# A new order of all steps in a gated FFT-convolution and MLP kernel, with the last output row in two pieces

## The chip, the cores and the metric

The kernel runs on one core of a Trainium2 chip. The metric is the device time of one execution in microseconds; several executions were timed, and their median counts. One further execution was recorded by the profiler, and all shares and durations below come from that one.

The engines are called as in the profile: PE is TensorE's matmul, PEld its weight load, DVE is VectorE, ACT is ScalarE, POOL is GpSimd and SP is SyncE, which in this kernel issues nearly all transfers (DMAs).

## The reference

The inputs have S = 2048 rows and D = 640 columns, and the MLP's inner width is F = 1536. All is bfloat16. `A_q` serves twice: as q of the first branch and as x of the second and of the gate.

```python
def _A_ref(q, k, v, shift_k, ssm_k, ssm_D):
    k_shift = sum(k_pad[:, t:t + S, :] * shift_k[:, ks - 1 - t] for t in range(4))   # four taps
    kv = k_shift * v
    kv_f, kf_f = rfft2(kv padded to 2S), rfft2(ssm_k padded to 2S)
    y = irfft2(kv_f * kf_f)[:S] + kv * ssm_D            # a convolution over all rows
    return q * y

def _B_ref(x, w1, w2, w3, w4):
    h = _gelu(_layernorm(x) @ w1)
    # four quarters of h's columns, shifted by +1, -1, +2, -2 rows
    x1 = x + concatenate([g0, g1, g2, g3]) @ w2
    return x1 + _gelu(_layernorm(x1) @ w3) @ w4

g = _sigmoid((x * gate_w).sum(-1))
out = g * _A_ref(...) + (1 - g) * _B_ref(...)
```

(The sum over taps and the padding are shortened here.)

## The kernel before

**Layout.** The 2048 rows stand as 128 partitions with 16 rows (`t1`) each; x, k, q and the output are worked on in four groups of four rows each (`c` = 0 to 3), 640 KB per group.

**Branch A.** `k_load` (L553) loads a group of k, and TensorE transposes it in three pieces (`transposed`, L618). `tap` (L574) makes the four-tap shift as products with diagonal matrices (`DG`) and multiplies by v. `v_load` loads v with indirect DMAs issued by POOL. The convolution is a Fourier transform in two stages, made of products with tables. `step1` (L409) is the first stage for kv (named `step1.KV.c`) and for the filter (`step1.HT0.c`, after `load_h` and `h_transpose`). Each step1 group makes two rows of 640 KB in SBUF, which are sent to DRAM (`S_x`, `S_h`; L434). `gather` (L437) reads them back in another arrangement. `step2` (L445) is the second stage, `product` (L479) multiplies the two spectra, `step3` (L494) goes back, again by way of DRAM (`S_g`), `gin` (L526) reads that, and `step4` (L861) makes the last stage and multiplies by q and by the gate.

**Branch B.** `x_stats` and `x_norm` make the layernorm: mean and variance on DVE or ACT, the power -1/2 on POOL, the scaling on DVE or ACT. `x_turn` (L635) transposes the result, groups 0 and 1 on TensorE and groups 3 and 2 by a transposing DMA. `mlp1` (L699) is W1 with its GELU on ACT, `w2` (L781) adds x, `x1_norm` (L793) is the second layernorm with a transposing DMA, `w3` (L828) has the second GELU and `w4` (L847) the last product. `w4` for one row makes 12 products of 512 columns and 12 of 128 columns into one PSUM tile, and DVE then works `ps * (1 - g) + x1` over all 640 columns (L854). The last operation of a row is DVE's addition of branch A (L889, the last part of `step4`). `store` (L844) writes two rows.

**What sets the order.** Nothing is scheduled by a tool. Every function above is cut into numbered parts, and one long string, `ORDER` (L893), lists all parts as `name.arguments:part`. The parts are issued in that order, each engine takes its own instructions from it, and every engine works its queue strictly in order. So the string sets the queue of PE, DVE, ACT, POOL and SP all at once. A letter in the arguments (`V` or `A`) says whether DVE or ACT does an evacuation or a norm; `D` means a DMA.

Buffers are set by hand as well. `SLOTS` (L66) gives the buffer of each allocation of a ring, in the order of the string: `c` four PSUM banks, `m` two wider PSUM tiles, `row` four SBUF buffers of 640 KB, which serve the loads of k, the normed rows, the step1 rows and q, and some smaller rings.

```python
def send(r):                                   # step1: one of the two rows of a group, L434
    SP.dma_start(out=scr[:, r, o:o + 4 * D], in_=stg[r][:])
...
for e in names:                                # emit: one entry of ORDER after the other
    n, k = e.split(":")
    ...
```

The opening of the string before the change is: a warm-up of TensorE with products of zeros (`warm`, L222, 11 matmuls and four times 3), the loads of x group 0, k 3, k 1 and k 2, then the next x and k 0, and only then W1; transposes of k and the first taps; the first `mlp1` after them.

Of the kernel before, what the change touches and what calls it, by code (L numbers as in the profile page):

```python
# [10 lines left out]
ALU = mybir.AluOpType  # L11
# [5 lines left out]
P = 128  # L17
# [12 lines left out]
def pieces(width):  # L30

    o = 0
    res = []
    while o < width:
        w = min(512, width - o)
        res.append((o, w))
        o += w
    return res
# [3 lines left out]
def kernel(  # L42
# [24 lines left out]
        "c": "012310320123102130120132013021320321010231302301203120321302103120302130213023012301203102310230"  # L67
             "123013201230312312010132013013012031023302131203012213020132030210312031023301230213102321003212"
             "130120310230132103210232031130220313120132002132013201323100231103232010123302130213021302130132"
             "0012301230123013213",  # L70
        "m": "01010101010101010101010101010101010101010101010101010101010101010101",
        "row": "01230132013120023102130213012030213030301",
        "gt": "012312002103120123012301201",
        "xt": "010101",
        "gq": "01210212012021012012101210110120120",
        "ax": "0123021302310312",
        "hp": "01231302",
# [98 lines left out]
    def flat(x):  # L176
        return x.rearrange("p t d -> p (t d)")
# [665 lines left out]

    def store(u):  # L844
        SP.dma_start(out=o_rows[:, 2 * u * D:2 * u * D + 2 * D], in_=flat(X1[:, 2 * u:2 * u + 2, :]))

    def w4(t1):  # L847
        c, i = t1 // 4, t1 % 4
        ps = slot(psm, [P, D], F32, "ps4", "m", 2)
        for (o, w) in pieces(D):  # L850
            for f in range(FC):
                PE.matmul(ps[:, o:o + w], lhsT=st["gt", c, f // 4][:, f % 4, i * P:(i + 1) * P], rhs=st["W4"][:, f, o:o + w], start=(f == 0), stop=(f == FC - 1))  # L852
            yield
        V.scalar_tensor_tensor(out=X1[:, t1, :], in0=ps[:], scalar=OMG[:, t1:t1 + 1], in1=X1[:, t1, :], op0=ALU.mult, op1=ALU.add)  # L854
# [6 lines left out]
    def step4(t1, ev):  # L861
# [240 lines left out]
```

## Time and profile before

| | us |
|---|---|
| median of 3 runs | 239.57 (239.03 to 241.48) |
| the profiled execution | 239.24 |
| its span | 237.5 |
| PE busy | 224.6 (95%) |
| DVE busy | 194.7 (82%) |
| ACT busy | 174.0 (73%) |
| POOL busy | 16.9 (7%) |
| mean granted clock of TensorE | 1.00 |
| bytes moved by DMA | 57.06 MB, mean 240 GB/s |

How to read it: the span runs from the first to the last instruction that the profiler recorded; the 1.74 us between it and the time of the profiled execution lie outside. Busy time counts an engine's instructions, not the issuing of DMAs. A share of busy time is an average over stages with different limits; which wait ends last in a stage is read from that stage.

### The profile page before, as it was taken

To read this page: it belongs to the slowest core of one execution; us is meant where nothing else is said; L and a number is where in the kernel's file an instruction comes from. 1 tells how busy PE (TensorE), PEld (TensorE's weight loads), DVE (VectorE), ACT (ScalarE), POOL (GpSimd) and SP (SyncE) were. 2 spreads that over 40 slices of the span, in tenths; PEclk is the share of its full clock that TensorE was granted. 3 is DMA by queue.
4 is the path that set the end of the run, shared out by engine and by line. 5 is a ranking of instruction groups with operands and counts; after the bars stand their busy time and mean duration, and the time that the engine had idled before them with its cause. 6 is when DMAs were issued, how large, how long until landed. Compare 5 with 4: busy or idle time off the path is not lost.

```text
span 237.5 us, 5627 instructions
## 1 busy us (share of the span) xinstructions
PE 224.6 (95%) x2241; PEld 115.8 (49%) x2260; DVE 194.7 (82%) x458; ACT 174.0 (73%) x311; POOL 16.9 (7%) x34
## 2 busy tenths in 40 slices
PE   8986999999999999999999999999999999999791
PEld 3764655533755555444544343444444445456551
DVE  7996999998998999875798897686895988129793
ACT  4796999878887989999697887673698533547560
POOL 4415022000000200021200000000000000000000
PEclk9999999999999999999999999999999999999999
DMA  6999919761999699996899902499950456399672
GB/s 248 375 391 353 359 60 197 182 246 56 382 354 294 212 361 208 353 385 261 286 278 190 354 1 89 130 272 317 360 163 5 139 196 198 138 272 369 190 276 110
DMA packets 42743, 57.06 MB, mean 240 GB/s; under 512 B 20313, under 2 KB 35418, under 8 KB 42462
## 3 DMA queue, kind: packets, MB, share of 16 engines
q1 hardware_dynamic: 42142, 54.10, 71.3%
q0 software_dynamic: 576, 2.62, 2.8%
q8 instruction: 17, 0.28, 0.5%
q14 instruction: 8, 0.07, 0.1%
HBM read 34.42 MB, written 18.36 MB: 222 GB/s over the span
## 4 chain that ended last, share of the span: by engine, by line
PE 87%; DMA 5%; DVE 3%; issue 2%; ACT 1%; SPq 0%; ACTq 0%
PE ps L834 22%; PE ps L852 20%; PE psm L709 10%; PE psw L786 9%; PE ps L462 5%; DMA WA<-in_B_w_dram 5%; PE ps L875 4%; PE ps L422 4%; PE psk L590 3%; PE ps L509 3%; PE psz L227 3%; PE ps L424 3%; PE pst L395 2%; PE pst L618 1%; DVE X L854 1%
## 5 line engine op out<-in xcount | busy, mean ns | idle before, releaser
L852 PE MATMUL ps<-W,gt 128*128 128x128 bf16 (+1 forms) x370 | 54.7, 296 | 1.2 <-issue 0.8
L834 PE MATMUL ps<-x1t,W 128*128 128x512 bf16 x240 | 55.6, 380 | 0.0
L852 PEld LDWEIGHTS <-gt 128*128 128x128 bf16 x384 | 29.0, 98 | 25.2 <-issue 4.9
L834 PEld LDWEIGHTS <-W 128*128 128x128 bf16 x240 | 21.9, 98 | 28.5 <-issue 4.7
L369 ACT CAST gs<-ps 128x320 bf16<-128x320 f32 x40 | 14.9, 433 | 20.4 <-PE ps L509 14.0
L369 ACT CAST stg<-ps 128x512 bf16<-128x512 f32 x46 | 24.8, 594 | 6.7 <-PE ps L424 3.7
L839 ACT ACTIVATE gt<-ps 128x1024 bf16<-128x1024 f32 x24 | 24.7, 1036 | 3.9 <-PE ps L834 3.8
L709 PE MATMUL psm<-xt,WA 128*128 128x512 bf16 x100 | 23.5, 380 | 1.8 <-DMA WA<-in_B_w_dram 1.8
L371 DVE CAST stg<-ps 128x512 bf16<-128x512 f32 x34 | 22.5, 684 | 2.1 <-PE ps L422 1.3
L786 PE MATMUL psw<-WA,HT 128*128 128x128 bf16 (+1 forms) x112 | 21.1, 296 | 0.4 <-issue 0.2
L879 ACT ACTIVATE y<-ps,GS 128x320 bf16<-128x320 f32 x23 | 11.5, 527 | 8.7 <-PE ps L875 6.4
L369 ACT CAST hs<-ps 128x512 bf16<-128x512 f32 x25 | 13.6, 598 | 3.4 <-PE ps L462 3.4
L371 DVE CAST XS<-ps 128x512 bf16<-128x512 f32 x17 | 11.3, 685 | 5.6 <-PE ps L462 5.6
L369 ACT CAST XS<-ps 128x512 bf16<-128x512 f32 x23 | 12.6, 595 | 4.2 <-PE ps L462 4.1
L709 PEld LDWEIGHTS <-WA 128*128 128x128 bf16 x100 | 9.0, 98 | 13.3 <-DMA WA<-in_B_w_dram 2.0
L371 DVE CAST hs<-ps 128x512 bf16<-128x512 f32 x15 | 10.1, 688 | 6.6 <-PE ps L462 6.5
L371 DVE CAST gs<-ps 128x320 bf16<-128x320 f32 x24 | 11.1, 486 | 5.2 <-PE ps L509 4.7
L786 PEld LDWEIGHTS <-HT 128*128 128x128 bf16 x116 | 10.0, 98 | 10.5 <-issue 0.8
L854 DVE SCALAR_TENSOR_TENSOR X<-ps,OMG,X 128x640 bf16<-128x640 f32 x16 | 14.0, 877 | 0.6 <-PE ps L852 0.6
L462 PE MATMUL ps<-ax,CMP 64*32 64x512 bf16 (+3 forms) x512 | 12.9, 300 | 0.1
L885 DVE SCALAR_TENSOR_TENSOR q<-ps,GS,q 128x320 bf16<-128x320 f32 x9 | 4.8, 546 | 10.0 <-PE ps L875 10.0
L788 DVE SCALAR_TENSOR_TENSOR X<-psw,X 128x640 bf16<-128x640 f32 x16 | 12.9, 818 | 0.2
(150 smaller groups left out, 362.6 us busy)
## 6 DMA issues: line engine op xcount, KB each, us to landing
S_x<-stg SPq DMA_DIRECT2D x8, 640.0 KB
S_h<-stg SPq DMA_DIRECT2D x8, 640.0 KB
ax<-S_x SPq DMA_DIRECT2D x8, 640.0 KB
ax<-S_h SPq DMA_DIRECT2D x8, 640.0 KB
S_g<-gs SPq DMA_DIRECT2D x8, 640.0 KB
W<-in_B_w_dram SPq DMA_DIRECT2D x2, 1920.0 KB
kn<-in_A_k_dram SPq DMA_DIRECT2D x4, 640.0 KB
q<-in_A_q_dram SPq DMA_DIRECT2D x4, 640.0 KB
```

Source lines behind the costliest of these rows:

```text
L369: A.copy(out=dst, in_=src)
L371: V.tensor_copy(out=dst, in_=src)
L422: PE.matmul(ps[r][:], lhsT=F1N[:, r].rearrange("p a b -> p (a b)"), rhs=src[:, o + 512 * u:o + 512 * u + 512], start=True, stop=True)
L462: PE.matmul(ps[j][q:q + 32, lo - 512 * u:hi - 512 * u], lhsT=CMP[HALF[j], 8 * b + 4 * h + i, c, :], rhs=st[name, 2 * b + h][HALF[j], i, lo ...
L709: PE.matmul(ps[:, v, :].rearrange("p (a b) -> p a b", a=4), lhsT=W1N[:, k, 160 * f:160 * f + P] if f < 4 else W1M[:, k, :], rhs=xt[:, :, k ...
L786: PE.matmul(ps[:, o:o + w], lhsT=h_tile(f, t1), rhs=W2P[:, f, o:o + w], start=(f == 0), stop=(f == 4))
L788: V.scalar_tensor_tensor(out=X1[:, t1, :], in0=ps[:], scalar=1.0, in1=X[:, t1, :], op0=ALU.mult, op1=ALU.add, accum_out=S12[:, 0, t1:t1 + 1])
L834: PE.matmul(ps[:, u, :].rearrange("p (a b) -> p a b", a=4), lhsT=st["W3"][:, k, f * P:(f + 1) * P], rhs=xt[:, :, k, :], start=(k == 0), st ...
L839: A.activation(out=gt[:, 2 * (fp % 2):2 * (fp % 2) + 2, :], in_=ps[:], func=ACT.Gelu_apprx_tanh)
L852: PE.matmul(ps[:, o:o + w], lhsT=st["gt", c, f // 4][:, f % 4, i * P:(i + 1) * P], rhs=st["W4"][:, f, o:o + w], start=(f == 0), stop=(f == ...
L854: V.scalar_tensor_tensor(out=X1[:, t1, :], in0=ps[:], scalar=OMG[:, t1:t1 + 1], in1=X1[:, t1, :], op0=ALU.mult, op1=ALU.add)
L879: A.activation(out=box["y"][:], in_=box["ps"][:], func=ACT.Copy, scale=GS[:, t1:t1 + 1])
```

## The change

Three things are changed.

1. The string `ORDER` is written anew from the first entry to the last. The parts are the same, apart from the last row of `w4` and one more store. The choice of engine (`V` or `A`) of many evacuations changes with it. In the opening, the loads are issued as x group 0, x group 1, k 3, W1, k 1, k 2, x 3, k 0; the layernorm, turning and W1 products of x group 0 stand ahead of most of k's transposes and of all taps; W2's load comes much later; `load_q.2` stands in the middle of the kernel, among the gathers. `gather.x.6` stands ahead of the first send of `step1.HT0.3`, and the transposing load of `x1_norm.0` ahead of the second.
2. `SLOTS` is written anew to go with it.
3. `w4` for row 14 (`LAST`) uses two single PSUM banks, one for 512 and one for 128 columns, and has an operation of its own for each on DVE; and `store` writes the last two rows one by one.

The opening of the string and the places that are spoken of, before and after:

```diff
-  "... load_x0.0:0 ... load_x0.1:0 ... k_load.3.AAA:0 ... k_load.1.VAA:0 ... k_load.2.VAV:0 ... load_cj:0 ... load_x.1:0 k_load.0.AVV:0
-   ... tap.7.AA:0 ... load_w1:0 ... tap.9.VA:0 load_x.3:0 ... mlp1.0.1:0 ... load_w2:0 ... tap.5.AV:0 ... mlp1.0.0:0 ..."
+  "... load_x0.0:0 consts0:0 consts0:1 warm:0 load_x0.1:0 load_x.1:0 ... x_norm.0.AVVA:0 f4_table:0 k_load.3.AAA:0 ...
+   load_w1:0 k_load.1.VVA:0 ... x_turn.0.AAA:0 ... k_load.3.AAA:1 k_load.2.AVA:0 ... mlp1.0.0:0 ... mlp1.0.1:0 ... tap.7.AA:0 ..."
...
-  "step1.HT0.2.AAVAVAVAVA:16 ... gather.x.1:0 ... step1.HT0.3.AVAVAAVAAA:16 ... :15 ... x1_norm.0.AVVA:6 ... gather.x.7:0 ... gather.x.0:0 gather.x.6:0"
+  "step1.HT0.2.AAAAAVAAAA:16 ... gather.x.1:0 ... gather.x.6:0 ... step1.HT0.3.AVAAAAAAAA:16 ... x1_norm.0.VVVV:6 ... step1.HT0.3.AVAAAAAAAA:15"
...
-  "... w4.14:0 ... store.3:0 store.5:0 ... w4.14:1 ... store.4:0 ... w4.14:2 step4.14.AA:6 store.6:0 store.7:0"
+  "... store.7:0 step4.13.AA:6 step4.12.AA:6 step4.14.AA:5 store.4:0 store.6:0 w4.14:0 w4.14:1 w4.14:2 w4.14:3 step4.14.AA:6 store.8:0"
```

and the code:

```diff
+    LAST = NT - 2
+
     def store(u):
-        SP.dma_start(out=o_rows[:, 2 * u * D:2 * u * D + 2 * D], in_=flat(X1[:, 2 * u:2 * u + 2, :]))
+        a, n = (2 * u, 2) if u < 7 else (22 - u, 1)
+        SP.dma_start(out=o_rows[:, a * D:(a + n) * D], in_=flat(X1[:, a:a + n, :]))

     def w4(t1):
         c, i = t1 // 4, t1 % 4
-        ps = slot(psm, [P, D], F32, "ps4", "m", 2)
+        ps = None if t1 == LAST else slot(psm, [P, D], F32, "ps4", "m", 2)
         for (o, w) in pieces(D):
+            to = slot(psc, [P, w], F32, "ps4", "c", 4) if ps is None else ps[:, o:o + w]
             for f in range(FC):
-                PE.matmul(ps[:, o:o + w], ...)
+                PE.matmul(to[:, 0:w], ...)
             yield
-        V.scalar_tensor_tensor(out=X1[:, t1, :], in0=ps[:], scalar=OMG[:, t1:t1 + 1], in1=X1[:, t1, :], op0=ALU.mult, op1=ALU.add)
+            if ps is None:
+                V.scalar_tensor_tensor(out=X1[:, t1, o:o + w], in0=to[:], scalar=OMG[:, t1:t1 + 1], in1=X1[:, t1, o:o + w], op0=ALU.mult, op1=ALU.add)
+                if o == 0:
+                    yield
+        if ps is not None:
+            V.scalar_tensor_tensor(out=X1[:, t1, :], in0=ps[:], scalar=OMG[:, t1:t1 + 1], in1=X1[:, t1, :], op0=ALU.mult, op1=ALU.add)
```

More of the change, by code (lines that the diff above doesn't have):

```diff
@@ L66 @@
     SLOTS = {
[L67 to L73, printed above, removed]
+        "c": "012301230213012310323103120132103123010320130213102321032103230120312013201320132031203102313201"
+             "203213021021323013203210312300123120231203123012130120313021323013223102103120310321032013212032"
+             "310230121303120301202130321231030122103032101231302031230123210123012031203103220133012301231023"
+             "103120312031201023102",
+        "m": "0100100101010101010101010101010101011010101010110101010101011010101",
+        "row": "01230121032130301230123102310320230202023",
+        "gt": "012301202120103102012301201",
         "xt": "010101",
-        "gq": "01210212012021012012101210110120120",
-        "ax": "0123021302310312",
-        "hp": "01231302",
+        "gq": "012201201102102101202102102101102101",
+        "ax": "0123023102130213",
+        "hp": "01231203",
     }
@@ L842, in scale_x1 @@
         scaled(ev, X1[:, t1, :], X1[:, t1, :], OMG[:, t1:t1 + 1])
+    LAST = NT - 2
     def store(u):
-        SP.dma_start(out=o_rows[:, 2 * u * D:2 * u * D + 2 * D], in_=flat(X1[:, 2 * u:2 * u + 2, :]))
+        a, n = (2 * u, 2) if u < 7 else (22 - u, 1)
+        SP.dma_start(out=o_rows[:, a * D:(a + n) * D], in_=flat(X1[:, a:a + n, :]))
     def w4(t1):
         c, i = t1 // 4, t1 % 4
-        ps = slot(psm, [P, D], F32, "ps4", "m", 2)
+        ps = None if t1 == LAST else slot(psm, [P, D], F32, "ps4", "m", 2)
         for (o, w) in pieces(D):
+            to = slot(psc, [P, w], F32, "ps4", "c", 4) if ps is None else ps[:, o:o + w]
             for f in range(FC):
-                PE.matmul(ps[:, o:o + w], lhsT=st["gt", c, f // 4][:, f % 4, i * P:(i + 1) * P], rhs=st["W4"][:, f, o:o + w], start=(f == 0), stop=(f == FC - 1))
+                PE.matmul(to[:, 0:w], lhsT=st["gt", c, f // 4][:, f % 4, i * P:(i + 1) * P], rhs=st["W4"][:, f, o:o + w], start=(f == 0), stop=(f == FC - 1))
             yield
-        V.scalar_tensor_tensor(out=X1[:, t1, :], in0=ps[:], scalar=OMG[:, t1:t1 + 1], in1=X1[:, t1, :], op0=ALU.mult, op1=ALU.add)
+            if ps is None:
[4 more added lines that the diff above has]
+            V.scalar_tensor_tensor(out=X1[:, t1, :], in0=ps[:], scalar=OMG[:, t1:t1 + 1], in1=X1[:, t1, :], op0=ALU.mult, op1=ALU.add)
     def load_q(c):
```

306 rows, old and new, of the table ORDER are left out of this document.

## The prediction

> **What bounds the kernel now.** I read the page's busy shares first, then the waits of TensorE, then windows of time, and then single instructions where the change moves something.
>
> ```profile
> PE 224.6 (95%) x2241; PEld 115.8 (49%) x2260; DVE 194.7 (82%) x458; ACT 174.0 (73%) x311; POOL 16.9 (7%) x34
> ...
> PE 87%; DMA 5%; DVE 3%; issue 2%; ACT 1%; SPq 0%; ACTq 0%
> ```
>
> TensorE (PE) is busy for 224.6 of 237.5 us and holds 87% of the chain that ended last. The change removes no product, so it can win only what PE now loses, and it can lose wherever a new wait stops PE. The waits of PE say where it stands still:
>
> ```profile
> PE psm L709 <- DMA WA<-in_B_w_dram: 1.8, 1, 1.8
> PE ps L875 <- DVE q L885: 1.2, 1, 1.2
> PE psz L227 <- DVE NPI L244: 1.0, 1, 1.0
> ...
> PE psk L590 <- ACT yk L598: 0.5, 1, 0.5
> ```
>
> There are two waits of size: 1.8 us for W1's load (WA) at 20.05, and 1.2 us in the last phase for DVE's gating of q. The rest of the loss is work without a product (warm-up matmuls, L227) and the tail after PE's last matmul. The windows (us; then busy PE, PEld, DVE, ACT, POOL, granted clock, share of DMA, GB/s):
>
> ```profile
> 10.00:20.00 10.00, 6.96 (x108) 5.61 (x105) 9.40 (x29) 9.84 (x16) 2.48 (x3) 1.00 1.03 392
> 20.00:30.00 10.00, 9.44 (x116) 6.36 (x117) 7.43 (x18) 7.51 (x14) 2.98 (x4) 1.00 1.04 344
> 30.00:60.00 30.00, 29.84 (x250) 13.50 (x250) 28.20 (x93) 26.77 (x49) 2.65 (x4) 1.00 0.57 152
> 60.00:76.00 16.00, 15.87 (x156) 10.52 (x156) 15.07 (x31) 12.88 (x22) 0.20 (x1) 1.00 1.02 364
> 76.00:95.00 19.00, 18.89 (x121) 9.95 (x121) 18.40 (x48) 17.79 (x37) 1.22 (x2) 1.00 0.86 246
> 95.00:120.00 25.00, 24.80 (x272) 11.15 (x273) 18.60 (x48) 22.45 (x40) 3.67 (x6) 1.00 0.91 323
> ```
>
> Three things stand here. PE loses 3 us of 10 in 10-20 and is full afterwards. DVE and ACT are also nearly full from 30 to 95, so a wait there is not made up by them. The DMA engines are saturated until 30 and again from 60 on, so the order of transfers decides when they land.
>
> **The opening (largest gain).** Before: by 26.29 us PE has done 100 transposes at 0.057 us (5.7), five taps of 22 matmuls at 0.92 (4.6) and ten W1 matmuls (2.3): 12.6 us of useful work, 13.7 us lost. From there to the q wait the loss grows no further. After: the loads are issued in the order x rows 0-3, next x, a k piece, then W1 (before: W1 was ninth, issued 9.27, landed 20.00). By the landing rate of before (640 KB in about 1.75 us) W1 lands near 11. The chain ahead of the first W1 product is then the layernorm: DVE's variance to 7.7, POOL's two rows (1.01 and 0.25 with gaps, to 9.3), four norms of 0.45 to 0.95 us on DVE and ACT (the first done at 10.3, the last near 11.5), 20 transposes, and the xt copies (1.02 and 0.60 us on ACT, 0.64 on DVE) to 13.3. Beside it PE does 40 transposes (2.3 us). So PE starts the W1 products at 13.35 with 2.3 us useful done: 11.05 lost against 13.7. In the next 13 us the taps' copies and the last x and k turns give waits like the rows of 0.3 to 0.5 us; I leave 0.4 for one. **-2.3** (-3.0 to -0.8). The four v loads go behind the third norm on POOL; the KV products that need them come after 30 us, which covers their 10 us. W2's load moves behind the transposing loads on SP; it is wanted some 5 us after its landing.
>
> **KV row 2 and the transposes of h.** The steps KV.2 with parts 9, 0 and 12 and the first transposes of h now stand back to back. The PSUM banks come round every 0.32 us (two 64-row matmuls), while a bank needs its evacuation (0.594 us on ACT, 0.684 on DVE) and two engines free a bank only every 0.32. The zero-row copies and four KV.1 copies stand ahead on ACT. Before, W2 products of 1.4 us lay between. Ends: 0, if the engines have caught up, and 1.0, two evacuations less the matmuls beside them; **+0.5**.
>
> **The row buffer at HT0.1.** Each 640-KB row of step1 (L409) is evacuated into one of four row buffers and sent from there. Before, this gave one wait, on ACT:
>
> ```profile
> L369 ACT CAST stg<-ps 128x512 bf16<-128x512 f32 x46 | 24.8, 594 | 6.7 <-PE ps L424 3.7 <-PE ps L422 1.7 <-DMA S_h<-stg 0.8
> ```
>
> It is the 0.82 us to 88.88, when the first send of HT0.3 had landed (88.80), and PE did not feel it. After, `gather.x.6` is issued ahead of that send: one more 640 KB, 1.75 us. And both engines now wait for the same buffer, DVE for part 11 and ACT for part 14. All sends are earlier by 2.3 - 0.5 = 1.8, so the buffer comes free near the old 88.8 (to 89.5), while PE is 1.8 ahead and wants it at about 87. PE has some 1.4 us of matmuls until it needs the bank; then the evacuation itself (0.69) is on the path: 88.8 - 87 - 1.4 + 0.69 = 1.1. Ends: 0 (as before) and 2.8 (one slower transfer more). The old row cost PE nothing, so I go below the middle: **+0.8**. What stands behind, the transposing load of `x1_norm.0` (landed 92.61, wanted 94.33) and gathers h.6 and h.7 (landed 116.53 and 118.34, wanted 117.69 and 118.86), has 0.5 to 1.7 us of slack that this stop gives back; 0 there.
>
> **The last phase.** `load_q.2` was issued at 212.53, behind the gin loads, and landed at 220.93; PE waited 1.23 at 220.4. Now it is issued near 125 and the wait goes. Against it, `load_q.0` and `gin.0.1` stand on SP between the last S_g send and `gin.0.2`, which the next step4 wants: 0 to 1.0 later, I take 0.3. The row `q.3` is wanted later than it lands by about 0.5. DVE's 8.23 of 10 us in 212-222 leaves a little for the moved gating; 0.2. -1.2 + 0.5 = **-0.7** (-1.2 to +0.5).
>
> **The tail.** Now the chain after PE's last matmul at 232.50 is:
>
> ```profile
> 232.53 0.88 DVE L854 SCALAR_TENSOR_TENSOR X<-ps,OMG,X 128x640 bf16<-128x640 f32 x1 [0.30 <-PE ps L852]
> 233.45 0.49 DVE L889 TENSOR_TENSOR X<-X,q 128x640 bf16<-128x640 bf16 x1
> ```
>
> then a store of 320 KB (issued 233.97, landed 236.13). Split, the 512-column operation lies beside the twelve 128-column matmuls (0.67 us), and only the 128-column one (estimate 0.3, from 0.877 for 640 and 0.546 for 320 columns) stays: -0.57. The last store holds one row, 160 KB: about -0.3 of its 2.16. **-0.9** (-0.5 to -1.1).
>
> **Evacuations** moved from DVE to ACT: about nine, 0.684 off DVE and 0.594 onto ACT each. PE has the same instructions. In the fullest stretch, 76-95, ACT has 1.2 us free and DVE 0.6, which covers the one or two that fall there; if it did not, each would cost what it takes on ACT. Priced at nothing beside the two terms above.
>
> Sum: 239.24 - 2.3 + 0.5 + 0.8 - 0.7 - 0.9 = 236.6. The profiled execution (span 237.5 and 1.74 outside it) is 0.33 below the median of 239.57; in its terms 237.0. A measurement of this kernel tells about 1% from no change, and 237.0 lies just below the 237.2 where that begins.
>
> **A rule on the clock.** All of this row's windows have a granted clock of 1.00, and the 1.81 us without a matmul at 18.2-20.05 were followed by ten W1 matmuls in 2.33 us, full pace. In the change the warm-up ends near 8.4, PE stands until 10.3 (1.9 us), and does only 2.3 us of small transposes in the next 3. If that cools the array, the first W1 products run at the pace of the first ten warm-up matmuls, which took 4.3 us (0.426 each; the next ten 0.215 each): ten or so of them, +2.1. The Trainium skill, "TensorE: Matmul & The Clock Gate", Part 1, says that the array falls back to half clock after an idle window of about 3.4 us, and rises after as long a busy one. By that rule 1.9 us alone keep it warm, as the trace of before agrees, but the sparse 5 us might not.
>
> **Rivals.**
> 1. The row buffer costs its whole price, 2.5 instead of 0.8: 238.7. For it: both evacuating engines stop at once and are over 93% busy there. Against: DMA has 14% free in 76-95. Chance 0.18.
> 2. The opening gains only 0.3: DVE and ACT are 94% and 98% busy in 10-20, and the W1 products add GELUs of 1.04 us to the same engines earlier. 239.0. Against: part of this work was there waiting, and PE's 13.35 is fixed by it already. Chance 0.10.
> 3. The clock falls in the opening: +2.1, 239.1. Chance 0.05.
> 4. Everything new hides (the +0.5 and +0.8 are 0): 235.7. Chance 0.06.
> 5. Slower: on SP the transposing load of `x1_norm.0` now stands ahead of HT0.3's second send. Before it held SP for 4.38 us (86.48 to 90.86), with that send ahead of it (issued 85.17, landed 90.34). If it holds SP as long, the send and all S_h sends behind it go 4 to 5 us later, into DMA queues that are full until 112; gathers h.6 and h.7 land near 121 to 123 instead of 116.5 and 118.3, and PE, with no slack there beyond 0.5 us, stands until then. The opening's gain is lost in it, and 4 us more: 239.24 + 4.2 - 0.7 - 0.9 = 241.8, 242.2 against the median. It decides from a landing of h.7 at 121 on; below it, the result is the forecast or rival 1. Against: the DMA queues are not empty during those 4.4 us, so what waits on SP loses less than that. Chance 0.16.
>
> **How the numbers follow.** The forecast has 0.45, of which 0.40 is below 237.2; with rival 4 that is 0.46 faster. Rivals 1 to 3 and the rest of the forecast make 0.38 within 1%. Rival 5 is 0.16 slower. Its own range: with the ends of the terms 234.9 to 239.0; the whole range reaches up to 241.2, leaving out most of rival 5, and down to 234.8.
>
> **What would show it.** Right: W1 landed near 11 and the first L709 at about 13.4; the wait on WA gone; no q wait above 0.5 us in step4; PE's last matmul within 0.5 us of the last 128-column STT. The row buffer would show as DVE and ACT idle on S_h near 88 and PE waiting on an evacuation there. Wrong: a first L709 after 15; PE idle over 2 us for a gather of S_h near 117; half-pace L709 at 13.

## The result, and the profile after

The changed kernel took 241.69 us (median of 14 runs, 241.15 to 242.78) against 239.59 us for the kernel before beside it: a ratio of 1.0091, 95% interval 1.0062 to 1.0119. In a later comparison (median of 4 runs) it was 242.98 us, ratio 1.0115 (1.0075 to 1.0155). The profiled execution took 241.72 us with a span of 239.9. The change made the kernel about 1% slower; 237.0 had been forecast, and the time lies above the range. The page of the changed kernel, busy time and the chain:

```profile
PE 227.0 (95%) x2260; PEld 115.2 (48%) x2260; DVE 191.6 (80%) x454; ACT 176.6 (74%) x318; POOL 17.6 (7%) x34
...
PE 71%; DMA 14%; ACT 8%; DVE 3%; issue 2%; POOL 1%; SPq 0%; ACTq 0%
```

PE held 87% of the chain before and holds 71% now; DMA and ACT have taken its place. The waits of PE (wait, sum, times, longest):

```profile
PE ps L422 <- ACT stg L369: 2.5, 3, 1.7
PE psz L227 <- DVE WZ L223: 1.9, 1, 1.9
PE pst L618 <- ACT xn L661: 1.6, 1, 1.6
PE ps L834 <- ACT gt L839: 1.0, 1, 1.0
...
PE ps L884 <- DMA gin<-S_g: 0.4, 1, 0.4
```

The two waits of before, for WA and for q, are gone. The new ones at the top and in the fourth line are in one place, as the windows show (same columns as before):

```profile
10.00:20.00 10.00, 9.90 (x107) 7.06 (x108) 9.64 (x31) 9.98 (x16) 4.32 (x6) 1.00 1.01 360
...
76.00:95.00 19.00, 16.54 (x105) 8.46 (x104) 14.11 (x38) 14.54 (x30) 1.78 (x2) 1.00 0.84 243
95.00:120.00 25.00, 23.78 (x231) 9.82 (x228) 18.31 (x42) 23.51 (x39) 2.43 (x4) 1.00 0.84 283
```

PE is busy for 9.90 of 10 us in 10-20, against 6.96 before. From 76 to 95 it has 16.54 of 19, against 18.89, and DVE and ACT too have fallen there, by 4.3 and 3.3 us. All three engines wait. The timeline of that place:

```profile
84.68 0.59 ACT L369 CAST stg<-ps 128x512 bf16<-128x512 f32 x1 [0.20 <-PE ps L422]
89.05 1.07 ACT L369 CAST stg<-ps 128x512 bf16<-128x512 f32 x2 [3.78 <-DMA S_h<-stg]
...
95.89 1.28 ACT L823 ACT_TABLE_LOAD   x1
...
100.20 1.28 ACT L839 ACT_TABLE_LOAD   x1
...
89.06 0.69 DVE L371 CAST stg<-ps 128x512 bf16<-128x512 f32 x1 [1.41 <-DMA S_h<-stg]
...
89.69 0.86 PE L422 MATMUL ps<-HT,F1N 128*128 128x512 bf16 x2 [1.68 <-ACT stg L369]
...
92.90 0.87 PE L422 MATMUL ps<-HT,F1N 128*128 128x512 bf16 x2 [0.56 <-ACT stg L369]
...
102.57 2.32 PE L834 MATMUL ps<-x1t,W 128*128 128x512 bf16 x10 [0.96 <-ACT gt L839]
```

ACT stands for 3.78 us until 89.05 and DVE for 1.41, both for the row buffer that the first send of HT0.3 still reads (issued 83.29, landed 88.97). PE stops 1.68 us later on. Then ACT is in arrears: PE waits for its copies at 92.90 and for its GELU at 102.57. And there is a line that the kernel before does not have: a table load for the Tanh of L823 at 95.89, with the GELU's own load after it at 100.20. In the kernel before the GELU's load came first, and the Tanh, behind it, had none:

```profile
96.39 1.28 ACT L839 ACT_TABLE_LOAD   x1
...
103.06 0.21 ACT L823 ACTIVATE GS<-ZG 128x16 f32<-128x16 f32 x1
```

To put numbers on places I use PE's lost time: the start of a step in the trace, less the durations of all PE work without the warm-up before it, each taken from the rows of before. It grows where PE stands or is slowed. Where the durations taken are a little too long it also falls slowly, in both kernels (from 13.19 to 11.44 between 122 and 200 in the kernel before), so only differences between kernels in the same row are read. (The stop in a pair of products is partly hidden in their longer modelled duration, 0.86 for 0.43, so lost time is more than the idle time in brackets.)

| after so much PE work (us) | before | after | after, second profile |
|---|---|---|---|
| 30 (opening) | 13.06 | 10.49 | 11.43 |
| 46, then 50 (KV.2) | 13.22, 12.90 | 10.56, 11.04 | 11.50, 11.99 |
| 76 | 13.23 | 11.37 | 12.29 |
| 78 (the stop) | 13.23 | 13.46 | 14.37 |
| 92 (its wake: what is lost behind it) | 13.60 | 16.52 | 17.43 |
| 122 | 13.19 | 16.82 | 17.63 |
| 200, then 216 (last phase) | 11.44, 12.34 | 15.13, 15.78 | 15.95, 17.05 |

(The second profile is that of the later comparison.) So 2.6 us are won in the opening (1.6 in the second profile), and 5.15 are lost between 76 and 92, where the kernel before lost 0.4.

### The profile page after: what moved, and what is told of

Its sections match the earlier page's. It is cut to its first block, busy times and chain, and to the rows that moved or that the text cites. A ratio compares the mean times of both kernels' runs of the same rounds, so it can differ in the third digit from the quotient of the medians.

```text
span 239.9 us, 5658 instructions
## 1 busy us (share of the span) xinstructions
PE 227.0 (95%) x2260; PEld 115.2 (48%) x2260; DVE 191.6 (80%) x454; ACT 176.6 (74%) x318; POOL 17.6 (7%) x34
## 4 chain that ended last, share of the span: by engine, by line
PE 71%; DMA 14%; ACT 8%; DVE 3%; issue 2%; POOL 1%; SPq 0%; ACTq 0%
PE ps L856 18%; PE ps L834 14%; PE psm L709 9%; DMA S_h<-stg 6%; PE psw L786 6%; PE psk L590 4%; PE ps L884 4%; PE ps L462 3%; PE pst L618 3%; PE ps L509 3%; ACT stg L369 3%; DMA ax<-S_h 3%; PE pst L395 2%; PE ps L422 2%; DMA gin<-S_g 2%
## 5 line engine op out<-in xcount | busy, mean ns | idle before, releaser
L856 PE MATMUL ps<-W,gt 128*128 128x512 bf16 (+1 forms) x384 | 56.8, 300 | 0.3 <-ACT gt L839 0.3
L369 ACT CAST stg<-ps 128x512 bf16<-128x512 f32 x56 | 29.8, 595 | 6.1 <-DMA S_h<-stg 3.8
L369 ACT CAST gs<-ps 128x320 bf16<-128x320 f32 x44 | 16.2, 440 | 18.8 <-PE ps L509 13.6
L371 DVE CAST stg<-ps 128x512 bf16<-128x512 f32 x24 | 15.9, 686 | 7.4 <-PE ps L422 3.6
L786 PE MATMUL psw<-WA,HT 128*128 128x512 bf16 (+1 forms) x116 | 21.7, 299 | 0.0
L369 ACT CAST hs<-ps 128x512 bf16<-128x512 f32 x25 | 13.5, 593 | 8.2 <-PE ps L462 8.2
L371 DVE CAST XS<-ps 128x512 bf16<-128x512 f32 x22 | 14.6, 685 | 4.4 <-PE ps L462 4.4
L786 PEld LDWEIGHTS <-HT 128*128 128x128 bf16 x116 | 10.0, 98 | 11.5 <-issue 2.5
L371 DVE CAST gs<-ps 128x320 bf16<-128x320 f32 x20 | 9.0, 485 | 7.8 <-PE ps L509 5.8
L422 PE MATMUL ps<-HT,F1N 128*128 128x512 bf16 x40 | 11.4, 379 | 2.7 <-ACT stg L369 2.5
L462 PE MATMUL ps<-ax,CMP 64*32 64x384 bf16 (+3 forms) x512 | 13.0, 300 | 0.2 <-DMA ax<-S_h 0.2
L712 ACT ACTIVATE HT<-psm 128x1024 bf16<-128x1024 f32 (+1 forms) x12 | 10.6, 895 | 2.4 <-PE psm L709 2.3
```

What stands on the lines that cost most here:

```text
L369: A.copy(out=dst, in_=src)
L371: V.tensor_copy(out=dst, in_=src)
L422: PE.matmul(ps[r][:], lhsT=F1N[:, r].rearrange("p a b -> p (a b)"), rhs=src[:, o + 512 * u:o + 512 * u + 512], start=True, stop=True)
L462: PE.matmul(ps[j][q:q + 32, lo - 512 * u:hi - 512 * u], lhsT=CMP[HALF[j], 8 * b + 4 * h + i, c, :], rhs=st[name, 2 * b + h][HALF[j], i, lo ...
L786: PE.matmul(ps[:, o:o + w], lhsT=h_tile(f, t1), rhs=W2P[:, f, o:o + w], start=(f == 0), stop=(f == 4))
L856: PE.matmul(to[:, 0:w], lhsT=st["gt", c, f // 4][:, f % 4, i * P:(i + 1) * P], rhs=st["W4"][:, f, o:o + w], start=(f == 0), stop=(f == FC ...
```

## The experiments

Ratios are to the kernel before, with the 95% interval; it took 240.07 to 240.34 us beside these runs. They were made in three sets, each with its own runs of the kernel before; times out of different sets are compared only roughly.

**One send behind one gather.**

```diff
-  ... gather.x.1:0 ... gather.x.6:0 ... step1.HT0.3.AVAAAAAAAA:16 ...
+  ... gather.x.1:0 ... step1.HT0.3.AVAAAAAAAA:16 gather.x.6:0 ...
```

> The changed kernel (241.69) with gather.x.6 issued behind the first send of step1.HT0.3 instead of ahead of it; nothing else. Theory W (the wait for the row buffer makes the loss): that send lands 1.75 us earlier, near 87.2; ACT's wait of 3.78 us shrinks to about 2, PE's first stop of 1.68 to near 0, and part of the wake behind it goes: 238.8 to 239.8. Rival A (ACT has too much work from 86 to 106 whatever the wait): 241.2. Rival D (the S_h gathers h.6 and h.7 set the pace near 117 to 122): PE gains and stands there instead, 241.0.

Measured: 241.05 us, ratio 1.0024 (0.9997 to 1.0051); the changed kernel's two medians lie 0.6 and 1.9 us above it. ACT's wait is cut to half, as expected, and the lost time between 76 and 92 falls from 5.15 to 3.20:

```profile
88.11 1.07 ACT L369 CAST stg<-ps 128x512 bf16<-128x512 f32 x2 [1.82 <-DMA S_h<-stg]
```

The wait is 1.96 us shorter, near the 1.75 of one 640-KB transfer. The time misses the 238.8 to 239.8 expected and is what the two rivals had given (241.2 and 241.0), so the time alone does not choose. In the trace PE waits only 0.2 us for h.6 and h.7, which speaks against rival D; rival A is left to the next experiment.

**A fifth row buffer.**

```diff
-  stg[r] = slot(ring, [P, 4 * D], BF16, "stg", "row", ROW)
+  if (name, c, r) == ("HT0", 1, 1):
+      stg[r] = pool("C").tile([P, 4 * D], BF16, name="stg5", tag="stg5", bufs=1)
+  else:
+      stg[r] = slot(ring, [P, 4 * D], BF16, "stg", "row", ROW)
```

> The changed kernel with a fifth row buffer: the second row of step1.HT0.1 goes to a buffer of its own, so no copy waits for the send of HT0.3; the order is untouched. Theory W: the waits of 3.78 us on ACT and 1.41 on DVE for S_h go, PE's 1.68 goes and most of the 3.1 us that PE loses behind it: 237.0 to 238.2, less if h.6 and h.7 then bind. Rival A: only the 1.7 goes, 240.0. Rival D: PE waits 3 us or more for h.6 and h.7, 240.5 or more.

Measured: 239.19 us, ratio 0.9948 (0.9919 to 0.9977). Nothing but the buffer is changed (and its entry in `SLOTS` taken out), and the time is 2.5 us under the first median of the changed kernel and 3.8 under the second. The window:

```profile
76.00:95.00 19.00, 18.89 (x121) 9.94 (x121) 16.54 (x42) 18.28 (x37) 1.78 (x2) 1.00 1.01 276
```

PE has its 18.89 us back, and the lost time grows by 1.36 between 76 and 92 instead of 5.15: 3.8 us less, where rival A gave 1.7. Theory W holds in the trace. ACT is busy for 18.28 of these 19 us, so it has next to no room for work left over from a wait; DVE, which gave some of its copies to ACT in the change, has more (16.54). The time is above the 237.0 to 238.2 expected; the trace shows the difference in the opening (11.5 instead of 10.5 lost in this profile) and in the last phase (below).

**The gate's Tanh behind the first GELU.**

```diff
-  ... gate:1 ... w3.0.2:1 ...
+  ... w3.0.2:1 gate:1 ...
```

> The changed kernel with one entry moved: gate:1 (the Tanh of L823) behind the first GELU of w3 instead of ahead of it, where the kernel before had it. The extra ACT_TABLE_LOAD of 1.28 us at 95.89 goes; the row wait stays. Theory W with the wake caused by ACT's arrears: PE loses 1 to 1.3 us less, 240.4 to 240.7. If ACT catches up anyway (the wake is the row wait's alone): 241.5.

Measured: 243.27 us, ratio 1.0103 (1.0043 to 1.0162), no gain. But the trace shows that it did its part: the load at 95.89 is gone, and the lost time between 76 and 92 is 3.80 instead of 5.15. That was given back further on. The time of 240.4 to 240.7 was not reached. The waits for S_h:

```profile
ACT stg L369 <- DMA S_h<-stg: 3.7, 1, 3.7
...
DVE stg L371 <- DMA S_h<-stg: 1.3, 1, 1.3
PE ps L462 <- DMA ax<-S_h: 1.2, 2, 0.8
```

In the changed kernel PE waited 0.2 us for the gathers h.6 and h.7 (`ax<-S_h`); now it waits 1.2. The stop at the row buffer had made the S_h sends late: the last one landed at 115.89, as in the second profile of the changed kernel (115.94), and at 112.44 in the next experiment, which has no stop. So h.6 and h.7 stood next in line.

**Both.** The fifth row buffer and the moved Tanh in one kernel.

> Both: fifth row buffer for step1.HT0.1 and gate:1 behind the first GELU. Theory W plus the table load: the 5.3 us that PE loses between 80 and 105 falls under 1; what is left is what the gathers of S_h allow: 236.5 to 237.5. If the two act on the same loss only once: as e2_fifth_row. Rival D: no better than 239.5.

Measured: 239.13 us, ratio 0.9924 (0.9897 to 0.9952). Lost time between 76 and 92: 0.36, as little as in the kernel before, so the buffer and the Tanh together are the whole loss there. The 236.5 to 237.5 expected was missed: against the fifth buffer alone the time is the same within its interval. From 92 to 122 1.3 us are lost, of which PE's waits for h.6 and h.7 are 1.1:

```profile
PE ps L465 <- DMA ax<-S_h: 1.1, 2, 0.6
```

Set side by side, the changed kernel and these four runs say what a stop of ACT costs here. Less the 0.4 of the kernel before, the loss between 76 and 92 is 4.8, 2.8 and 1.0 us for an ACT wait of 3.78, 1.82 and 0 with the Tanh ahead of the GELU, and 3.4 and 0 for a wait of 3.7 and 0 with it behind. So PE lost about as much as ACT had stood, and the Tanh's load added 1.0 to 1.4.

**The send ahead of the transposing load.** This tests the last rival of the prediction.

```diff
-  ... x1_norm.0.VVVV:6 ... step1.HT0.3.AVAAAAAAAA:15 ...
+  ... step1.HT0.3.AVAAAAAAAA:15 x1_norm.0.VVVV:6 ...
```

> The changed kernel with the second send of step1.HT0.3 issued ahead of the transposing load of x1_norm.0, as before the change, instead of behind it. The last rival of the prediction (that load holds SP, and all S_h sends and the gathers h.6 and h.7 come late): 1.5 to 3 us faster than the changed kernel. Theory W (nobody waits for that send's row before HT0.0, and PE is so late itself that h.6 and h.7 cost it 0.2 us): within 0.5 us of it, ratio to the kernel before 1.006 to 1.011.

Measured: 242.78 us, ratio 1.0108 (1.0074 to 1.0143); ACT's wait stayed at 3.7 us, and the ratio lies where theory W had it. The rival came near the time (242.2), but neither its place (PE standing for h.6 and h.7 near 117, where it waited 0.2 us) nor its cause was right; the nearness is luck.

**Two small losses at once.** With the fifth buffer and the gate, `w2.15` was put between KV.2's parts, and `load_q.0` behind `gin.0.2`.

```diff
-  ... w2.15:0 ... step1.KV.2.VAAAAVAVAA:2 step1.KV.2.VAAAAVAVAA:12 ...   load_q.0:0 ... gin.0.1:0 ... gin.0.2:0
+  ... step1.KV.2.VAAAAVAVAA:2 w2.15:0 step1.KV.2.VAAAAVAVAA:12 ...       gin.0.1:0 ... gin.0.2:0 load_q.0:0
```

> Fifth row buffer and gate:1 behind the first GELU, and with them w2.15 between step1.KV.2's parts 0 and 12 (for the 0.8 us lost there) and load_q.0 behind gin.0.2 (for the 0.8 us that gin.0.2 lands later than it must). If the two losses are what the trace shows them to be: 1 to 1.5 us below e9_row_and_gate (ratio 0.9924 to the kernel before), ratio 0.986 to 0.988. If the time comes back as waits for S_h at h.6 and h.7: ratio 0.990 or more.

Measured: 239.85 us, ratio 0.9988 (0.9959 to 1.0018), slower than without, where 0.986 to 0.988 had been expected. Lost time at 50 us of PE work is 12.91 instead of 12.24, so the new spacing made KV.2 worse: `w2.15` had stood between two groups of KV products, and without it PE is slowed there (four of them take 1.84 us, from 57.40, instead of 0.68). Moving `load_q.0` cut the loss from 200 to 204 from 1.2 to 0.3, and from 208 to 212 0.7 came back.

**q's first group early, in the fifth buffer.** With the fifth buffer and the Tanh moved; KV.2 as in the changed kernel.

```diff
+  if c == 0:
+      q2 = pool("C").tile([P, 4, D], BF16, name="q5", tag="stg5", bufs=1)
...
-  ... load_q.2:0 ... load_q.0:0 ... gin.0.1:0 ... gin.0.2:0 ...
+  ... load_q.2:0 load_q.0:0 ... gin.0.1:0 ... gin.0.2:0 ...
```

> e9_row_and_gate (fifth row buffer, gate:1 behind the first GELU) with q's first group loaded early into the fifth buffer, which is free after step1.HT0.1's send, instead of between the last S_g send and gin.0.2. gin.0.2 then lands 0.8 to 0.9 us earlier, and q 0 is there long before. If that wait is gin.0.2's alone: 0.8 us below e9_row_and_gate, ratio 0.988 to 0.990. If DVE's work on q sets the last phase (in e10_all PE lost 0.7 later what it had won): no change, 0.992.

Measured: 238.16 us, 4.8 us under the changed kernel in the same comparison (242.98); ratio 0.9923 (0.9897 to 0.9949). `gin.0.2` was on its way for 4.55 us instead of 5.38, the wait for it is gone, and the lost time at the end is 11.96 instead of 13.26, less than the 12.26 of the kernel before. The ratio does not separate it from the version without (0.9924, in another set) and is the one expected for no change; the trace does separate them. It is the fastest version by its median.

**Copies of z_rows on DVE.**

```diff
-  A.copy(out=zr[32 * c:32 * c + 1, :], in_=ps[32 * c:32 * c + 1, :])
+  (A.copy if c < 2 else V.tensor_copy)(out=zr[32 * c:32 * c + 1, :], in_=ps[32 * c:32 * c + 1, :])
```

> e11_q_early with two of the four copies of z_rows (L725, 2.34 us in a row on ACT) on DVE. Theory Z (these copies keep KV.2's banks waiting, not the nearness of the KV.2 parts): the 0.5 to 0.9 us that PE loses between 54 and 60 go, and another 0.3 to 0.7 us of the time if h.6 and h.7 do not take them back. Rival: DVE is as full there, no change.

Measured: 239.78 us, ratio 0.9989 (0.9961 to 1.0017), 1.6 us slower than the version without, in the same set. Its waits say who is late now:

```profile
PE ps L424 <- DVE stg L371: 1.8, 2, 1.3
```

DVE had no room for the two copies, while ACT was busy only 6.48 of the 10 us from 50 to 60 (8.52 without). Theory Z is neither shown nor refuted by this. What would take away the 0.5 to 0.8 us at KV.2 stays open.

**The opening: load and order apart.** First the kernel before with W1's load fourth, the order of the work untouched.

```diff
-  ... k_load.1.VAA:0 ... load_w1:0 ...
+  ... load_w1:0 k_load.1.VAA:0 ...
```

> The kernel before with one entry moved: W1's load is issued ahead of k 1 (fourth transfer) instead of ninth, with the order of the work as it was. Theory O (the opening is won by the order of the work, the load alone is not enough): the wait of 1.8 us for WA goes, but k 1 and k 2 land 2 us later, where PE's work of that time is k's transposes; net -0.5 to +1.5 us. Rival L (the load is what was late): 1.5 to 1.8 us faster, ratio near 0.993.

Measured: 240.63 us, ratio 1.0027 (0.9992 to 1.0063). The wait for WA is gone, and another stands at its place:

```profile
PE pst L618 <- DMA kn<-in_A_k_dram: 3.9, 4, 1.8
```

Then the changed kernel with W1's load two transfers later:

```diff
-  ... load_w1:0 k_load.1.VVA:0 ... k_load.2.AVA:0 ...
+  ... k_load.1.VVA:0 ... k_load.2.AVA:0 load_w1:0 ...
```

> The changed kernel with W1's load behind k 1 and k 2, the work in the changed order. W1 lands near 14.2 instead of 10.8, while its first product is wanted at 13.2: PE stands 1 us there, k 1 and k 2 come earlier. If the place of the load is what the order of the work needs: PE's loss at 26 us grows by 0.8 to 1.2, time +0.5 to +1.2, ratio 1.011 to 1.014. If the opening is bound by DVE and ACT (9.6 and 10.0 us busy of 10 in 10-20): no change, 1.009.

Measured: 245.04 us, ratio 1.0211 (1.0172 to 1.025), 2.1 us over the changed kernel in the same set, more than the 0.5 to 1.2 expected. W1 landed at 15.12 instead of 10.96, PE stood for 2.28 us until 15.16, and the lost time at 30 is 13.44 instead of 11.43. So the order and the load win together, neither alone.

**The tail alone.** The kernel before with the last row as in the change.

```diff
+  (w4, store and LAST as in the change)
-  w4.14:1 ... store.4:0 step4.15.AA:6 w4.14:2 step4.14.AA:6 store.6:0 store.7:0
+  ... store.4:0 step4.15.AA:6 store.7:0 store.6:0 w4.14:1 w4.14:2 w4.14:3 step4.14.AA:6 store.8:0
```

> The kernel before with the change's last row alone: w4 of row 14 in two pieces with two operations on DVE, the last two rows stored one by one. By the tail's working of the prediction (-0.57 for the operation, -0.3 for the store): 0.5 to 1.1 us faster, ratio 0.9955 to 0.998. Rival (the store's latency does not depend on its size, and DVE's start costs eat the rest): 0.3 us or less, ratio above 0.9985.

Measured: 239.90 us, ratio 0.9967 (0.9925 to 1.0008), which alone decides nothing. In the trace, span less lost time at the last row is 224.6 against 225.2 before, 0.7 us less before rounding. In the changed kernel it is 224.2, 1.0 us less. The last store, now of one row, landed 1.8 us after its issue in both, instead of 2.16. The tail of the changed kernel:

```profile
235.30 1.02 DVE L859 SCALAR_TENSOR_TENSOR X<-ps,OMG,X 128x512 bf16<-128x512 f32 x2
236.35 0.49 DVE L898 TENSOR_TENSOR X<-X,q 128x640 bf16<-128x640 bf16 x1
```

**The changed kernel again**, in the set of q's early load, the z_rows copies and the later W1.

> The changed kernel itself once more, as the mate of the three others. Theory W: 1.0091 as in the first comparison, within 0.3%; the opening loses 10.5 to 11.6 us of PE's time, the row wait and its wake 5 us.

Measured: 242.98 us, ratio 1.0115; the loss between 76 and 92 is 5.1 us again.

## Why the prediction was wrong, point by point

- **The opening**, -2.3 (-3.0 to -0.8): -2.6 in the first profile, -1.6 in the second. W1 landed at 10.81 (forecast: near 11), and the first W1 product began at 13.20 (forecast 13.35). Right in its working. The first profile flatters it: the nine later ones with this opening all win 0.9 to 1.2 us less, and all show a wait of 0.8 to 1.0 us of PE for DVE's copies of xt that the first does not have.
- **The clock**: the first ten W1 products took 2.32 us, the full pace, after PE had stood for 1.64 us. The rival on it fell.

```profile
10.07 0.62 PE L618 MATMUL pst<-IDB,xn 128*128 128x128 bf16 x8 [1.64 <-ACT xn L661]
...
13.20 2.32 PE L709 MATMUL psm<-xt,WA 128*128 128x512 bf16 x10
```

  The rule of the Trainium skill, "TensorE: Matmul & The Clock Gate", Part 1, in the reading that a rest well under its window keeps the array warm, agrees with this trace. The granted clock would not have told: it reads 1.00 also from 0.9 to 5.2 us before the change, where the warm-up products took 0.426 each; the pace of the products tells.
- **KV.2**, +0.5: +0.8 by the table (11.04 - 10.56, where the kernel before fell by 0.3). Inside its ends. Its cause, the nearness of the parts, was not confirmed: moving them apart by one product made it worse.
- **The row buffer at HT0.1**, +0.8 (0 to 2.8): this is the term that failed. The mechanism was the one that was described (that send behind `gather.x.6`, landing forecast 88.8 to 89.5, measured 88.97; both engines wait for one buffer). The size was not. The place lost 5.15 us against 0.4 before, +4.8, of which the buffer is 3.4 to 3.8 by the experiments and the Tanh the rest. The first stop of PE was 1.7 to 2.1, inside the ends given. Behind it came the wake: ACT and DVE had been busy for over 93% of that window before the change, ACT could not make up the work for which it had stood, and PE waited for it at three more places. The prediction had written just this fullness down ("a wait there is not made up by them"), and then let PE's own 1.4 us of matmuls hide part of the wait and priced the stop alone, below the middle because of one row that had cost nothing; what counted was ACT's wait of 3.78, which it did not work out. The rival on it, with 2.5, was too low for the same reason.
- **The gate's Tanh** is missing from the prediction. `gate:1` stood behind the GELU before, where the Tanh (0.21 us) used the table that was there; ahead of it, it brings a load of 1.28 us onto ACT in the middle of the wake. The trace with it moved loses 1.35 us less there, and 1.0 less where the wait for the buffer is gone too. The Trainium skill, "ScalarE: Activation LUTs", Table sets, says that tables are loaded by sets and that work should be grouped by them, and its section "What ACT_TABLE_LOAD costs" gives about 1.28 us for the load and 2.66 us with a drain for each switch of sets. The trace agrees on the load (1.28 us) and shows no idle time of ACT for a drain around it: the load begins at 95.89, 0.02 us after the end of the work before it, and the Tanh at 97.19, 0.01 us after the load.
- **Evacuations**, 0: ten of step1's copies went from DVE to ACT (46 became 56). With the buffer and the Tanh mended and the copies as in the change, the place loses 0.36, so they cost nothing by themselves. They left ACT fuller (18.28 of 19 us in the run with the fifth buffer, 17.79 before); that this made the wait dearer is argued, not tested.
- **What stands behind**, 0: the slack of h.6 and h.7 was given back as forecast while PE was late (0.2 us of wait), and became a wait of 0.9 to 1.3 in the five runs with the Tanh moved, where PE came earlier to it.
- **The last phase**, -0.7: -0.25 by the table, +0.2 in the second profile. The 1.2 us for q went; `gin.0.2`, on its way behind `load_q.0`, landed 5.0 us after its issue, before 4.2, and PE waited 0.4 and 1.0 us for it in the two profiles (0.8 to 1.5 of lost time from 200 to 204), where 0.3 was priced.
- **The tail**, -0.9: -0.7 to -1.0. Right.
- **The range.** The ends of the five terms, all taken together, reach from 5.3 below to 3.0 above, in the median's terms 234.3 to 242.6. The range was drawn narrower at its upper end (241.2), to leave out most of the last rival.

By the table: -2.6 + 0.8 + 4.8 + 0.8 (92 to 200, not forecast; no run separates it) - 0.25 - 1.0 = +2.5, and the profiled execution is 2.5 us longer. The forecast's sum of -2.6 and this one differ by 5.1 us: the place of the row buffer makes 4.0 of that, 2.6 to 3.0 by the buffer itself and the rest by the Tanh.

The last rival (slower, 242.2) named SP, held by a transposing load, as the cause. SP was held for 3.67 us by it, the send did go late (89.23, before 85.17), and nobody waited for it.

```profile
85.52 3.67 SPq L813 DMA_TRANSPOSE x1t<-xn  x1
```

Its sign did come: h.7 landed at 121.89, behind the 121 that it had named. But PE was as late itself and waited 0.2 us, and with the send ahead of that load (the run above) h.7 landed at 122.99, no earlier than in the second profile of the changed kernel (122.71).

## What to carry to other kernels

Where an engine that empties PSUM is nearly full, a wait that stops it costs PE more than the first stop: the work not done in the wait comes late too. Here PE lost about as much as ACT had stood (3.4 to 3.8 us for 3.7 to 3.8, 1.8 for 1.8), so the length of the engine's wait was the price, not PE's first stop; that is one place of one kernel. In an order written by hand, look at each transfer that is moved ahead of a send whose buffer is wanted next. And when an activation is moved past another, look at which table it finds.

## What the runs showed of the hardware that was not expected

- The opening of the kernel before varies. In the run with the tail alone, which has the same opening, W1 landed at 21.72 instead of 20.00, PE waited 3.1 us instead of 1.8, and lost 16.1 us at 20 us of PE work instead of 13.5. In the first comparison 13 of the 14 runs of the kernel before lie between 238.12 and 241.48 us, and those of the changed one between 241.15 and 242.78. What makes the opening vary stays open.
- `x1_norm`'s transposing loads held SP's queue for 3.7 us at 85.52 and for 7.5 us at 118.18, in the changed kernel; four gathers were on their way ahead of the second.
- A Tanh behind the GELU needed no table load; ahead of it, it brought a load of 1.28 us.
